# Fused forgetting attention and channel mix on one core: PSUM copies moved to ScalarE, and every slot ordered by a list from an offline model

## The chip, the cores and the metric

The kernel runs on one core of a Trainium2 chip. The metric is device time in microseconds (us): the median of several executions. The profile's span, from the first to the last instruction, is 1 to 2 us shorter than the time. Executions are compared only where they ran at about the same granted clock, the share of full speed at which TensorE was allowed to run (the fast state), and each kernel's runs are interleaved with runs of the kernel before on the same chip.

## The reference

Eight batches, eight heads, 576 positions, head size 64. A causal attention with a forget gate feeds a channel mix of 512 to 1024 to 512.

```python
scores = scale * np.matmul(q, k.transpose(0, 1, 3, 2))
cum = np.cumsum(np.log(np.clip(f, 0.0001, 1.0)), axis=-1)
scores = np.where(causal, -1e9, scores + cum[..., :, None] - cum[..., None, :])
attn = softmax(scores);  x = (attn @ v), heads side by side          # (8, 576, 512)
x_prev = x shifted by one position
xk = mu_k * x + (1 - mu_k) * x_prev;   xr = mu_r * x + (1 - mu_r) * x_prev
k = np.maximum(xk @ w_k, 0.0)
return sigmoid(xr @ w_r) * ((k * k) @ w_v)
```

## The kernel before

The order of instructions on each engine is the order in which the program writes them: nothing is rescheduled afterwards. Work goes in **slots**, one for each of the 32 pairs of heads (four pairs make a batch), and three more to empty the pipeline. A slot computes the scores and exponentials of its own pair, transposes q and k of the next one, casts those of the one after, sums the denominators of the previous pair, multiplies the values of a pair that lies three slots back, and runs key, gate and value units of the channel mix of an earlier batch between them.

Three scarce things tie the engines together: two score buffers in PSUM (`sc`, which also take the transposes), three general PSUM buffers (`mm`, for values, key, gate and value units), and three buffers `rb` for the normaliser, which travels through DRAM.

```python
sc_ring = Ring(2, [P, 2, 512], F32, "sc", scp)
mm_ring = Ring(3, [P, 512], F32, "mm", mmp)
rb_ring = Ring(3, [P, 2, S], F32, "rb")
...
def transposes(Pi, parts=(range(NC),)):         # TensorE, then the copy out of PSUM
    tp = sc_ring().bitcast(BF16)
    ...
            if Pi < RUNS and lo == 0:           # first six pairs: a strided copy
                nc.vector.tensor_copy(t[:, :, 0:4 * P].rearrange(...), tp[:, :, 0:4 * P].rearrange(...))
                lo = 4 * P
            if lo < hi:
                nc.vector.tensor_copy(t[:, :, lo:hi], tp[:, :, lo:hi])
...
def spread_norm(g):                             # R -> DRAM -> broadcast into rb
    scr = scr_ring()
    nc.sync.dma_start(out=scr..., in_=R...)
    rb = rb_ring()
    for half in range(2):
        for hh in range(2):
            nc.sync.dma_start(out=rb[...], in_=scr[2 * half + hh, 0:2, :].unsqueeze(0).to_broadcast([D, 2, HQ]))
...
def values(Pi, half):                           # TensorE into mm, then the product x = mm * rb
    ...
    nc.vector.tensor_tensor(out=xs[Pi % NX][...], in0=nm[:, 0:HQ], in1=rbs[Pi][...], op=ALU.mult)
...
def shift(Pi):                                  # the token shift: three VectorE instructions in SBUF
    nc.vector.tensor_sub(diff, x[:, 1:S + 1], x[:, 0:S])
    for dst, mu in ((xks[b], mu_k_sb), (xrs[b], mu_r_sb)):
        nc.vector.scalar_tensor_tensor(out=dst[:, p, :], in0=diff, scalar=mu[:, p:p + 1],
                                       in1=x[:, 0:S], op0=ALU.mult, op1=ALU.add)
...
def key_unit(b, hf, fb):                        # TensorE into mm, relu on ScalarE, square on VectorE
    kp = mm_ring()
    ...
    nc.scalar.activation(rel, kp[:, :HB], func=AF.Relu)
    nc.vector.tensor_mul(rsq[b][:, fb, hf * HB:(hf + 1) * HB], rel, rel)
...
def value_unit(b, t0):                          # TensorE into mm, product with the gate on VectorE
    ...
    nc.vector.scalar_tensor_tensor(out=res, in0=gates.pop((b, t0)), scalar=1.0, in1=vp, op0=ALU.add, op1=ALU.mult)
```

GpSimd casts q and k (`cast_pair`, and once a batch `cast_tails` for the last 64 positions), weights v with the gates (`vw_pair`, once a batch `vw_tail`) and masks. From slot 6 on, every slot has this one order:

```python
scores_and_masks(s, 0); run_gv(value_unit); transposes(s + 1)
run_keys(nk[0]); scores_and_masks(s, 1); cast_ahead(s)
denominators(s - 1); attend(Pi)                 # values of the pair three back
weigh(Pi); norm(...)                            # norm and its spreading in even slots
run_keys(nk[1]); spread_norm(...); shifted(Pi)
run_gv(); ...                                   # gate and value units
```

The softmax here doesn't subtract the row's maximum and nothing guards it: scores larger than these inputs give would overflow.

## Time and profile before

Before: 332.34 us, median of three runs (331.99 to 333.09). The span of its profile is 331.3 us.

I use one ruler: the start of each of the 32 groups of transposes on TensorE, numbered from 0. Between group 9 and group 31 every kernel of this study runs the same units (85 key units, 24 gate and value pairs, 22 slots of attention; the kernels with lists run six score matmuls more, about 0.5 us), so that stretch can be compared directly. I call it the **steady stage**; groups 1 to 9 are the **warm-up**, group 31 to the end the **drain**.

| stage of before | us |
|---|---|
| to group 1 | 13.5 |
| warm-up, groups 1 to 9 | 54.4 |
| steady, groups 9 to 31 | 197.8 |
| drain | 65.7 |

The busy times by stretch, before. The first column is the stretch in us from the span's start; then its length and the busy time of each engine with the count of its instructions; the last three are the granted clock of TensorE, the share of the DMA engines and GB/s.

```profile
core 0: us, PE busy (x) PEld busy (x) DVE busy (x) ACT busy (x) POOL busy (x), PEclk, DMA share, GB/s
13.50:67.87 54.37, 39.23 (x417) 24.26 (x418) 36.47 (x64) 32.06 (x49) 38.55 (x71) 0.94 0.88 170
67.87:265.63 197.76, 178.42 (x1852) 103.98 (x1852) 153.45 (x278) 116.35 (x198) 111.86 (x193) 0.99 0.76 171
```

Read the second row as a balance: 197.8 us long, TensorE busy for 178.4, so idle for 19.3.

VectorE's costliest SBUF work, before, by shape; the two numbers after the bar are us busy in all and ns of one.

```profile
L419 DVE TENSOR_TENSOR relusq<-rel 128x288 bf16<-128x288 bf16 x128 | 59.1, 484 | 12.1 <-ACT rel L418 10.2
L403 DVE SCALAR_TENSOR_TENSOR xk<-diff,mu_k_sb,x 128x576 bf16<-128x576 bf16 x32 | 28.5, 890 | 1.1
L401 DVE TENSOR_TENSOR diff<-x 128x576 bf16<-128x576 bf16 x32 | 18.2, 570 | 0.1
```

All three have two inputs in SBUF. Undisturbed, with no GpSimd instruction beside them, they take 0.31, 0.82 and 0.45 us (medians in this trace); their means here are well above that, which matters later.

### The profile page before, as it was taken

The page shows a single profiled execution, that of the slowest core. Times are in us where ns is not written, and L with a number is a line of the kernel's source. Part 1 is how long each engine was busy: PE and PEld are TensorE (multiplying, and loading weights), DVE is VectorE, ACT ScalarE, POOL GpSimd, SP SyncE. Part 2 cuts the span into 40 slices and gives each one's busy share as a digit, 9 for nine tenths or more (in the row PEclk, how much of TensorE's full clock was granted, in tenths as well). Part 3 has the DMA queues.
Part 4 walks back from the last instruction along what each step waited for, and adds up shares of the span by engine and source line. Part 5 has one row for each costly group of instructions (what it writes and reads, how often), then busy time and mean ns, then how long its engine had stood idle before and what let it go on. Part 6 is the DMA issues. An engine that isn't in the chain of part 4 may idle for free.

```text
span 331.3 us, 7464 instructions
## 1 busy us (share of the span) xinstructions
PE 278.4 (84%) x2741; PEld 162.8 (49%) x2741; DVE 235.2 (71%) x443; ACT 179.3 (54%) x304; POOL 165.3 (50%) x298
## 2 busy tenths in 40 slices
PE   1477668769979889899979897998889897989995
PEld 0235345445545535455545554554455554654552
DVE  4746567996888659777888778685888785677531
ACT  1655347656646646475746565575656574332541
POOL 6269655984684618445664547264745456000000
PEclk9999789999999979999999999999999999999999
DMA  8998997394968494946876696819595615041012
GB/s 180 239 206 174 189 202 133 95 204 125 217 156 209 115 214 111 256 93 164 213 188 157 157 220 165 228 55 217 137 240 109 163 55 168 32 153 64 34 63 96
DMA packets 123172, 51.33 MB, mean 155 GB/s; under 512 B 104384, under 2 KB 117952, under 8 KB 123136
## 3 DMA queue, kind: packets, MB, share of 16 engines
q1 hardware_dynamic: 120160, 47.70, 62.6%
q0 software_dynamic: 2096, 2.62, 4.8%
q10 hardware_dynamic: 880, 0.54, 0.7%
q8 instruction: 21, 0.34, 0.4%
q14 instruction: 15, 0.12, 0.1%
HBM read 41.96 MB, written 11.50 MB: 161 GB/s over the span
## 4 chain that ended last, share of the span: by engine, by line
PE 52%; DVE 21%; DMA 17%; SPq 4%; issue 3%; ACT 1%; POOL 1%; ACTq 0%; DVEq 0%; POOLq 0%
PE mm L426 21%; DMA rb<-scr 11%; PE mm L414 10%; PE mm L378 6%; PE sc L296 5%; SPq L349 4%; PE sc L229 4%; DMA scr<-R 4%; PE den L327 4%; DVE relusq L419 3%; DVE x L385 3%; DVE xr L403 2%; DVE qkT L237 2%; DVE qkT L233 2%; DMA rb<-in_f_dram 2%
## 5 line engine op out<-in xcount | busy, mean ns | idle before, releaser
L309 POOL TENSOR_SCALAR_AFFINE_SELECT a<-a 128x256 bf16<-128x256 bf16 (+1 forms) x160 | 73.7, 483 | 113.8 <-ACT a L302 108.8
L302 ACT ACTIVATE a<-sc 128x1024 bf16<-128x1024 f32 (+1 forms) x128 | 101.4, 836 | 19.1 <-PE sc L296 17.9
L418 ACT ACTIVATE rel<-mm 128x288 bf16<-128x288 f32 x128 | 52.5, 410 | 77.0 <-PE mm L414 73.6
L414 PE MATMUL mm<-xk,wk_sb 128*128 128x288 bf16 x512 | 74.1, 286 | 3.9 <-DVE xk L403 1.7
L419 DVE TENSOR_TENSOR relusq<-rel 128x288 bf16<-128x288 bf16 x128 | 59.1, 484 | 12.1 <-ACT rel L418 10.2
L426 PE MATMUL mm<-wv_sb,relusq 128*128 128x512 bf16 x256 | 62.4, 385 | 3.4 <-DVE relusq L419 3.0
L385 DVE TENSOR_TENSOR x<-mm,rb 128x288 bf16<-128x288 f32 x64 | 29.3, 461 | 41.1 <-PE mm L378 17.8
L414 PEld LDWEIGHTS <-wk_sb 128*128 128x128 bf16 x512 | 46.7, 98 | 19.4 <-issue 5.8
L296 PE MATMUL sc<-qkT 64*128 64x64 bf16 (+4 forms) x384 | 39.3, 293 | 18.5 <-DVE qkT L237 17.6
L440 ACT ACTIVATE th<-mm 128x512 f32<-128x512 f32 x36 | 21.5, 597 | 40.1 <-PE mm L426 34.2
L447 DVE SCALAR_TENSOR_TENSOR res<-th,mm 128x512 f32<-128x512 f32 x36 | 24.6, 682 | 24.7 <-ACT a L302 10.0
L426 PEld LDWEIGHTS <-relusq 128*128 128x128 bf16 x256 | 23.7, 99 | 35.1 <-issue 6.4
L426 PE MATMUL mm<-wr_sb,xr 128*128 128x512 bf16 x128 | 32.8, 379 | 7.2 <-DVE x L385 7.2
L296 PEld LDWEIGHTS <-qkT 64*128 64x128 bf16 x384 | 16.3, 96 | 45.3 <-issue 39.8
L211 POOL TENSOR_TENSOR vw<-vf,wbf 128x512 bf16<-128x512 f32 x32 | 34.3, 1072 | 1.5 <-DMA vf<-in_v_dram 1.5
L378 PE MATMUL mm<-a,vw 128*64 128x288 bf16 (+3 forms) x448 | 29.0, 269 | 1.0 <-DVE x L385 0.5
L403 DVE SCALAR_TENSOR_TENSOR xk<-diff,mu_k_sb,x 128x576 bf16<-128x576 bf16 x32 | 28.5, 890 | 1.1
L403 DVE SCALAR_TENSOR_TENSOR xr<-diff,mu_r_sb,x 128x576 bf16<-128x576 bf16 x32 | 27.9, 873 | 0.0
L327 PE MATMUL den<-a,E 128*2 128x288 bf16 (+4 forms) x512 | 22.7, 258 | 0.6 <-DVE E L268 0.5
L237 DVE COPY qkT<-sc 128x1280 bf16<-128x1280 bf16 (+1 forms) x32 | 22.8, 713 | 0.4 <-PE sc L229 0.4
L378 PEld LDWEIGHTS <-vw 128*64 128x64 bf16 x448 | 19.4, 113 | 7.5 <-issue 1.6
L426 PEld LDWEIGHTS <-xr 128*128 128x128 bf16 x128 | 12.4, 97 | 19.2 <-issue 9.1
(63 smaller groups left out, 242.7 us busy)
## 6 DMA issues: line engine op xcount, KB each, us to landing
out_dram<-res SPq DMA_DIRECT2D x36, 256.0 KB, 3.3
vf<-in_v_dram SPq DMA_DIRECT2D x64, 128.0 KB, 3.6
rb<-scr SPq DMA_DIRECT2D x56, 144.0 KB, 3.4
qf<-in_q_dram SPq DMA_DIRECT2D x52, 128.0 KB, 3.7
kf<-in_k_dram SPq DMA_DIRECT2D x52, 128.0 KB, 3.7
scr<-R SPq DMA_DIRECT2D x14, 144.0 KB, 1.7
qf<-in_q_dram SPq DMA_DIRECT2D x6, 256.0 KB, 3.4
kf<-in_k_dram SPq DMA_DIRECT2D x5, 256.0 KB, 4.1
```

The lines of the kernel that those rows point to most:

```text
L211: nc.gpsimd.tensor_tensor(out=vw[Pi % NV], in0=vf[Pi % NV], in1=wbf[:, :4, 2 * Pi:2 * Pi + 2].unsqueeze(3).to_broadcast([P, 4, 2, D]), op= ...
L296: nc.tensor.matmul(sc[:, hh, w:w + n], lhsT=t[lo:lo + D, 1, kb * P:(kb + 1) * P], rhs=t[lo:lo + D, 0, q0:q0 + n], start=True, stop=True)
L302: nc.scalar.activation(out=a[:, :, off:off + w], in_=sc[:, :, 0:w], func=AF.Exp, scale=SCALE)
L309: nc.gpsimd.affine_select(out=v_, in_=v_, compare_op=ALU.is_ge, fill=0.0, base=0, pattern=[[0, 2], [1, n]], channel_multiplier=-1)
L327: nc.tensor.matmul(den[r0:r0 + 2, o:o + n], lhsT=E[:, kb, 2 * h:2 * h + 2], rhs=a[:, hh, col:col + n], start=(Pi % 2 == 0 and kb == 0), st ...
L378: nc.tensor.matmul(nm[hh * D:(hh + 1) * D, o:o + n], lhsT=t[:, kb, hh, :] if kb < 4 else tl[:, 2 * p + hh, :], rhs=a[:, hh, col:col + n], ...
L385: nc.vector.tensor_tensor(out=xs[Pi % NX][:, 1 + o:1 + o + HQ], in0=nm[:, 0:HQ], in1=rbs[Pi][:, o:o + HQ], op=ALU.mult)
L403: nc.vector.scalar_tensor_tensor(out=dst[:, p, :], in0=diff, scalar=mu[:, p:p + 1], in1=x[:, 0:S], op0=ALU.mult, op1=ALU.add)
L414: nc.tensor.matmul(kp[:, :HB], lhsT=wk_sb[:, db, fb * P:(fb + 1) * P], rhs=xks[b][:, db, hf * HB:(hf + 1) * HB], start=(db == 0), stop=(db ...
L418: nc.scalar.activation(rel, kp[:, :HB], func=AF.Relu)
L419: nc.vector.tensor_mul(rsq[b][:, fb, hf * HB:(hf + 1) * HB], rel, rel)
L426: nc.tensor.matmul(ps, lhsT=tiles[b][:, i, t0:t0 + P], rhs=w[:, i, :], start=(i == 0), stop=(i == n - 1))
```

## The change

There are three parts. The copy of transposed q and k out of PSUM goes from VectorE to ScalarE. The order within a slot is no longer one fixed sequence but a list of letters: one list for each of the first eleven slots, four that repeat, one for the drain; the lists come from an offline model of the engines. And at the start the gates are loaded first, their clamp stands ahead of the casts, and only the tails of the first two heads are loaded and cast before the first transposes.

```diff
+    nc.scalar.dma_start(out=lf, in_=f_bh[:, :])
     load(q, qf[0], 0)
     load(k, kf[0], 0, nc.scalar)
-    load_tail(0, 0)
-    load_tail(1, 0, nc.scalar)
-    nc.scalar.dma_start(out=lf, in_=f_bh[:, :])
+    load_tail(0, 0, hs=(0, 2))
+    load_tail(1, 0, nc.scalar, hs=(0, 2))
     load_qk(1)
+    load_tail(0, 0, hs=(2, H))
+    load_tail(1, 0, hs=(2, H))
...
             if Pi < RUNS and lo == 0:
-                nc.vector.tensor_copy(t[:, :, 0:4 * P].rearrange("p i (j c) -> p i j c", c=4),
+                nc.scalar.copy(t[:, :, 0:4 * P].rearrange("p i (j c) -> p i j c", c=4),
...
             if lo < hi:
-                nc.vector.tensor_copy(t[:, :, lo:hi], tp[:, :, lo:hi])
+                nc.scalar.copy(t[:, :, lo:hi], tp[:, :, lo:hi])
...
-    cast_pair(0)
     nc.vector.tensor_scalar(lf, lf, scalar1=1e-4, scalar2=1.0, op0=ALU.max, op1=ALU.min)
     nc.scalar.activation(out=lf, in_=lf, func=AF.Ln)
+    cast_pair(0)
...
+    FIRST = ( ...eleven lists... 
+        "T G S0 c K3 S1 D W N G A P H G",
+        ... )
+    ROUND = (
+        "S0 V G T V K2 S1 c G A K2 D W N P H R G",
+        "S0 V K3 V T D c K1 S1 V G A H R W",
+        "S0 G T D K2 S1 A N c K2 P W G H R",
+        "S0 V T G K3 A D S1 G c K1 W H R",
+    )
+    DRAIN = "D V W K4 A N K4 H G G G P R"
-    WEIGHTS = (1, 3, 4)
+    WEIGHTS = (1, 3, 5)
...
+    def step(s, op, x):          # one branch for each letter
...
+        for op in (FIRST[s] if s < len(FIRST) else ROUND[s % PRW] if s < NP else DRAIN).split():
+            step(s, op[0], int(op[1:]) if op[1:] else None)
```

The letters that the argument needs: S0 and S1 are the two halves of the scores with exponentials and masks, T the transposes and their copy, D denominators, A the values and their products, N the normaliser and P its trip through DRAM, H the token shift, K2 two key units, V a value unit, G the next gate or value unit, R the gate and value units left over; c the casts and W the weighting of v, both on GpSimd.

## The prediction

> **What bounds the kernel now.** I read the page first (busy shares, slices, chain), then the waits, then the groups by shape, then the engines' timelines from 0 to 70 us and from 127 to 163 us. From the page of the kernel before, busy shares, two slice rows and the chain by engine:
>
> ```profile
> PE 278.4 (84%) x2741; PEld 162.8 (49%) x2741; DVE 235.2 (71%) x443; ACT 179.3 (54%) x304; POOL 165.3 (50%) x298
> ...
> PE   1477668769979889899979897998889897989995
> ...
> DMA  8998997394968494946876696819595615041012
> ...
> PE 52%; DVE 21%; DMA 17%; SPq 4%; issue 3%; ACT 1%; POOL 1%; ACTq 0%; DVEq 0%; POOLq 0%
> ```
>
> TensorE leads, yet only half of the last-ending chain is its own work: VectorE and the round trip of the normaliser through DRAM take most of the rest, ScalarE almost nothing. The first six slices (50 us) are a stage of their own: TensorE at 4 to 8 tenths, the DMA engines at 8 to 9.
>
> 84% overstates TensorE. From the timelines of a dense stretch, back to back: a group of ten transposes takes 0.56 us, the two halves of the scores 0.54 and 0.36, denominators 0.58, values 0.83, a key unit 0.49 (the chain has eight of its matmuls in 0.98), a gate block 0.86, a value block 1.73. I took the start of each of the 32 transpose groups in TensorE's timeline as a clock of the slots. Group 9 starts at 67.87 and group 31 at 265.63: 197.8 us for 22 slots, 9.0 each. Inside lie 22 x 2.87 (transposes, scores, denominators, values), 85 key units x 0.49 and 24 gate and value pairs x 2.59 (three of them straddle two batches and run as column halves side by side: 16 of those matmuls take 1.85): 63.1 + 41.7 + 62.9 = 167.7 us. So **30 us, 1.37 per slot, are lost in the steady stage**. The fastest full slots do show it possible: 142.15 to 149.76 is 7.61 us without a gap.
>
> Where they are lost, from the waits (waiter, released by: us in total, times, longest):
>
> ```profile
> PE sc L296 <- DVE qkT L237: 17.6, 15, 2.9
> DVE x L385 <- DMA rb<-scr: 17.5, 15, 2.3
> PE mm L426 <- DVE x L385: 7.6, 9, 2.0
> DVE rb L245 <- DMA rb<-in_f_dram: 3.6, 1, 3.6
> ```
>
> The first is the copy of transposed q and k out of PSUM: two score buffers exist, the transposes occupy one, and the last small score piece has to wait until VectorE has emptied it. The timelines of VectorE and of TensorE around 133 us show why VectorE is late:
>
> ```profile
> 131.45 0.95 DVE L403 SCALAR_TENSOR_TENSOR xr<-diff,mu_r_sb,x 128x576 bf16<-128x576 bf16 x1
> 132.32 0.68 DVE L447 SCALAR_TENSOR_TENSOR res<-th,mm 128x512 f32<-128x512 f32 x1
> 132.92 0.81 DVE L237 COPY qkT<-sc 128x1280 bf16<-128x1280 bf16 x1
> ```
> ```profile
> 133.79 0.20 PE L296 MATMUL sc<-qkT 64*128 64x64 bf16 x2 [1.11 <-DVE qkT L237]
> ```
>
> The transposes were done at 130.4; the copy stood behind the token shift and an output product in VectorE's queue for 2.5 us, and TensorE idled 1.11 us.
>
> At the start, the clamp of the gates stands on VectorE ahead of the same copy and waits for its load:
>
> ```profile
> 8.74 0.45 DVE L245 TENSOR_SCALAR rb<-rb 64x576 f32<-64x576 f32 x1 [3.61 <-DMA rb<-in_f_dram]
> ...
> 9.12 1.21 DVE L233 COPY qkT<-sc 128x1024 bf16<-128x1024 bf16 x1
> ```
>
> The transposes had ended at 5.8, so about 3.3 us of the first 9 are this clamp.
>
> **What the Trainium skill says.** "Perfetto Trace Analysis", section Identifying the Most-Contended Engine: matmul busy time is no measure of headroom because matmuls are pipelined. The trace agrees: a 512-column matmul is shown as 0.38 us, but 16 of them take 3.45 us, 0.216 each. That is why I used spacing, not busy share. "ScalarE: Activation LUTs", section What ACT_TABLE_LOAD costs: an activation with immediate operands takes 186 ns + 0.833 ns per element, and neighbours overlap by some 93 ns. The trace agrees: 1023 ns for 1024 elements, 410 for 288, 274 for 128. "SBUF — State Buffer", section Who interferes with whom: a VectorE instruction with two SBUF inputs contends with GpSimd, one with at most one SBUF input does not, outside two-port modes. The trace agrees in part: the square of the keys takes 0.31 us at best and 0.48 on average. So the moved copy, whose input is in PSUM, is not what GpSimd suffers from, and I count no gain there.
>
> **The change part by part.**
>
> (1) *Copies to ScalarE.* VectorE loses 26 x 0.81 + 6 x 1.21 + 6 x 0.28 = 30 us, from 235 to 205. ScalarE gains 26 copies of 1280 elements (186 + 1066 = 1.25 us, estimate by the ScalarE page; its own rows give 1.23) and six pairs of 1024 and 256 (1.02 + 0.40, taking the strided read as free): 32.5 + 8.5 = 41 us, from 179 to 220. Each copy is longer by 0.4 us, but it no longer waits behind 2.5 us of token shift; it waits behind exponentials instead. Per steady slot ScalarE has 3.34 (exponentials) + 4 x 0.41 + 9/8 x 0.60 + 1.25 = 6.9 us, VectorE about 6.5, TensorE 4.83 + 9/8 x 2.59 = 7.7. TensorE stays the longest, with ScalarE now close behind.
>
> (2) *Operation lists.* The order of instructions shows the same units on TensorE, moved. In the steady slots the transposes come earlier and key units, values or gates stand between them and the second half of the scores, so the copy has 1 to 3 us of cover. The values that need a freshly spread normaliser come after more TensorE work: before, some 5.5 us passed between the norm and its use (147.3 to 152.8); in the new odd slot two value blocks, four key units, transposes, denominators and half of the scores lie between, and in the slot after the norm in mid-slot about 7, against a DRAM trip of 7 to 8 us (1.75 to store, 2 to issue, 3.5 to load). Of the 1.37 us lost per slot I expect half back, a judgement: the first three waits listed above sum to 43 us over the whole run, and each shrinks rather than goes. 22 x 0.69 = **15 us**.
>
> (3) *Warm-up, first exponential to group 9.* Groups 1 to 6 start at 13.5 and 50.0: 7.3 us per slot. ScalarE would be busy 3.34 + 1.42 + 0.82 (spreading on chip) = 5.6, GpSimd 5.0, so neither permits 5. TensorE's waits for the copy in this stretch sum to 0.85 + 1.04 + 1.50 + 2.94 + 2.56 + 0.59 = 9.5 us. The DMA engines were full here (1.0 or more of their time in the windows from 20 to 50 us), though the third weight now leaves one slot later. I take 5 of 9.5: **5 us**.
>
> (4) *Start.* The gates are loaded first, only two heads of the tails are needed, and the clamp comes ahead of the casts. Other loads landed 3.3 us after issue, so the clamp ends near 4.5, casts near 5.4, transposes 6.3, ScalarE's copies near 7.9. Then the second table load, which the before kernel hid beside copying, comes in series (1.28 us). First exponential near 9.3 instead of 11.93: **2.5 us**.
>
> (5) *Drain.* From group 31 to the end 65.7 us; its units are the same number (36 keys, 12 pairs, the last values) and sum to 54, plus 4 for the last product and store. The order changes a little: **1 us**.
>
> The sum is 15 + 5 + 2.5 + 1 = 23.5, so 332.3 - 23.5 = 308.8. An order computed from modelled durations loses some of its fit on the chip, so I keep nine tenths: 311.
>
> **The rivals.** *ScalarE becomes the bound.* Exponentials, relu, tanh and copies share one in-order queue; key units need relu to free one of three PSUM buffers. For it: 6.9 of 7.7 us per slot, and a copy ahead of three relus. Against it: 54% busy before. If it holds, half of (2) is lost: about 318. *DMA holds the warm-up and the rb round trip.* For it: full DMA engines to 50 us, chains through rb; a faster slot asks for the same bytes sooner. Against: hardly any wait there names a q, k or v load (2.2, 1.1 and 1.5 us). Then (3) is nothing and (2) shrinks: about 317. *The lists fit better than I allow*, steady slots at 8.1 us: (2) gives 20 us, about 304. *Nothing gained*: copies return as equal waits on ScalarE; only the start remains, 328.
>
> **Range and chances.** The two bad cases together (318 and 317, each 6 to 7 above 311) give near 323 and the good one 304; I set 302 to 322. I give 89% to faster, since a gain under 6.6 us would need (2) and (3) both almost to fail; 9% to the same, 2% to slower.
>
> **What would show it.** Right: the first exponential near 9.3 us; the copy rows on ScalarE at about 1.25 us; VectorE near 205 and ScalarE near 220 us busy; waits of scores on the copy under 6 us in total; group 9 near 60 us; groups 9 to 31 some 182 to 186 us apart. Wrong: long waits of key matmuls on relu or of transposes on exponentials (ScalarE the bound), products waiting for rb as long as before, masks or casts waiting on loads, or strided copies well above 1.02 us.

## The result and the profile after

The changed kernel takes **319.46 us**, median of four runs (318.76 to 319.84), against 332.16 for the kernel before in the same rounds (331.64 to 333.09). Ratios in this document are the mean time of one kernel's fast runs over the mean of the other's fast runs of the same rounds, so not quite the ratio of the medians: 0.9612, 95% interval 0.9585 to 0.9640. It is faster by 3.9%, within the predicted range; the predicted gain was 21.3 us, the measured one 12.7.

From the page of the kernel after: busy shares, TensorE and DMA slices, chain by engine.

```profile
PE 277.0 (87%) x2741; PEld 162.3 (51%) x2741; DVE 218.5 (69%) x407; ACT 213.0 (67%) x342; POOL 174.5 (55%) x298
...
PE   2675887598998998999988998999979999999994
...
DMA  8999959596968495928788696929695526141102
...
PE 62%; DVE 18%; ACT 7%; DMA 5%; issue 4%; POOL 2%; SPq 1%; DVEq 0%; ACTq 0%; POOLq 0%
```

VectorE lost 17 us, ScalarE gained 34. The DMA engines' part of the chain fell from 17% to 5%, but VectorE's only from 21% to 18%, although it gave its copies away.

The busy times by stretch, after, the same columns as before:

```profile
10.68:61.40 50.72, 36.87 (x411) 23.17 (x411) 28.63 (x49) 38.80 (x60) 39.25 (x68) 0.97 0.95 182
61.40:253.73 192.33, 179.55 (x1858) 104.43 (x1858) 143.73 (x255) 141.16 (x222) 120.11 (x195) 0.99 0.76 177
```

| stage | before | after | gain | predicted gain |
|---|---|---|---|---|
| to group 1 | 13.5 | 10.7 | 2.8 | 2.5 |
| warm-up | 54.4 | 50.7 | 3.7 | 5 |
| steady | 197.8 | 192.3 | **5.4** | **15** |
| drain | 65.7 | 63.4 | 2.3 | 1 |
| span | 331.3 | 317.1 | 14.2 | 23.5 |

Everything but the steady stage came out close. There TensorE's busy time is the same (178.4, 179.6), and its idle time went from 19.3 to 12.8 us. What it idles for, in the waits of TensorE over the steady stage (us in total, times, longest), before and then after:

```profile
PE sc L296 <- DVE qkT L237: 7.8, 8, 2.0
PE mm L426 <- DVE x L385: 5.1, 7, 2.0
PE mm L426 <- DVE relusq L419: 3.0, 3, 1.0
PE mm L414 <- DVE xk L403: 1.7, 2, 0.9
```
```profile
PE mm L418 <- DVE res L451: 5.6, 7, 1.2
PE sc L233 <- ACT a L306: 3.4, 4, 1.0
PE sc L300 <- ACT qkT L241: 2.0, 2, 1.0
PE mm L418 <- DVE xk L407: 1.3, 4, 0.3
```

The change did what it was made for: the scores' wait for the copy fell from 7.8 to 2.0 us, and the gate and value units no longer wait for products (5.1) or squares (3.0). But a wait that the kernel before did not have leads the list: key units waiting for an output product, `res`, 5.6 us. The timeline of the kernel after from 154 to 161 us shows where it is made (start, duration, engine, operation; the bracket is idle time and releaser):

```profile
154.52 0.76 POOL L204 CAST kb<-kf 128x512 bf16<-128x512 f32 x1
...
155.23 1.24 POOL L212 CAST tail<-tail_f 64x512 bf16<-64x512 f32 x2
...
155.36 1.42 DVE L405 TENSOR_TENSOR diff<-x 128x576 bf16<-128x576 bf16 x1
...
156.44 1.23 POOL L221 TENSOR_TENSOR tail<-tail_f,wbf 64x512 bf16<-64x512 f32 x1
156.81 2.48 DVE L407 SCALAR_TENSOR_TENSOR xk<-diff,mu_k_sb,x 128x576 bf16<-128x576 bf16 x1
...
160.09 0.68 DVE L451 SCALAR_TENSOR_TENSOR res<-th,mm 128x512 f32<-128x512 f32 x1
...
160.82 0.40 PE L418 MATMUL mm<-xk,wk_sb 128*128 128x288 bf16 x2 [1.19 <-DVE res L451]
```

The three instructions of the token shift take 0.45, 0.82 and 0.82 us undisturbed. Here, while GpSimd casts and weighs, `diff` takes 1.42 and `xk` 2.48 us; `xk` ends at 159.29, 0.6 us after GpSimd's weighting of v (157.64 to 158.68, among the lines left out). The output product behind it ends at 160.77; it held one of the three `mm` buffers, and the key unit that needed that buffer starts 0.05 us later after 1.19 us of idling. The same 1.19 us are lost just before 125, 195 and 231 us: once in every four slots, after the slot whose list ends in "N c K2 P W G H R", where the casts, the weighting and the tails of a batch fall beside the shift.

The groups say the same of the whole run (same columns as before):

```profile
L423 DVE TENSOR_TENSOR relusq<-rel 128x288 bf16<-128x288 bf16 x128 | 50.2, 408 | 30.2 <-ACT rel L422 28.6
L407 DVE SCALAR_TENSOR_TENSOR xk<-diff,mu_k_sb,x 128x576 bf16<-128x576 bf16 x32 | 34.7, 1084 | 1.1
L405 DVE TENSOR_TENSOR diff<-x 128x576 bf16<-128x576 bf16 x32 | 27.2, 852 | 0.4
```

`diff` rose from 570 to 852 ns and `xk` from 890 to 1084, `xr` from 873 to 1002; the squares fell from 484 to 408. The contention was moved from the squares to the shift. A count over the same trace shows that GpSimd is the cause: with no GpSimd instruction beside them, no `diff`, `xk`, `xr` or square took more than 457, 819, 814 or 310 ns; beside GpSimd work other than masks they took up to 2078, 2485, 2445 and 1864. In the kernel before, 4 of the 32 `diff` ran beside such work, after the change 24.

Two lines on the parts that went as predicted, ScalarE's copy by shape and then its timeline at the start:

```profile
L241 ACT COPY qkT<-sc 128x1280 bf16<-128x1280 bf16 x26 | 31.9, 1227 | 12.0 <-PE sc L233 11.3
```
```profile
8.31 1.28 ACT L306 ACT_TABLE_LOAD   x1
9.60 1.02 ACT L306 ACTIVATE a<-sc 128x1024 bf16<-128x1024 f32 x1
```

### The profile page after: what moved, and what is told of

It is laid out like the page before. It is cut to its first block, busy times and chain, and to the rows that moved or that the text cites. A ratio compares the mean times of both kernels' runs of the same rounds, so it can differ in the third digit from the quotient of the medians.

```text
span 317.1 us, 7414 instructions
## 1 busy us (share of the span) xinstructions
PE 277.0 (87%) x2741; PEld 162.3 (51%) x2741; DVE 218.5 (69%) x407; ACT 213.0 (67%) x342; POOL 174.5 (55%) x298
## 4 chain that ended last, share of the span: by engine, by line
PE 62%; DVE 18%; ACT 7%; DMA 5%; issue 4%; POOL 2%; SPq 1%; DVEq 0%; ACTq 0%; POOLq 0%
PE mm L430 20%; PE mm L418 16%; PE mm L382 7%; PE sc L300 6%; PE den L331 5%; PE sc L233 4%; PE mm L434 4%; ACT a L306 3%; DVE xr L407 3%; DVE diff L405 3%; DVE relusq L423 3%; DVE res L451 3%; DMA kf<-in_k_dram 2%; DVE xk L407 2%; DMA rb<-scr 1%
## 5 line engine op out<-in xcount | busy, mean ns | idle before, releaser
L313 POOL TENSOR_SCALAR_AFFINE_SELECT a<-a 128x256 bf16<-128x256 bf16 (+1 forms) x160 | 79.8, 520 | 92.9 <-ACT a L306 81.0
L306 ACT ACTIVATE a<-sc 128x1024 bf16<-128x1024 f32 (+1 forms) x128 | 100.1, 841 | 14.7 <-PE sc L300 14.6
L423 DVE TENSOR_TENSOR relusq<-rel 128x288 bf16<-128x288 bf16 x128 | 50.2, 408 | 30.2 <-ACT rel L422 28.6
L430 PE MATMUL mm<-wv_sb,relusq 128*128 128x512 bf16 x256 | 60.7, 380 | 0.0
L389 DVE TENSOR_TENSOR x<-mm,rb 128x288 bf16<-128x288 f32 x64 | 28.6, 459 | 30.7 <-PE mm L382 14.2
L300 PE MATMUL sc<-qkT 64*128 64x64 bf16 (+4 forms) x384 | 37.9, 290 | 8.9 <-ACT qkT L241 5.9
L241 ACT COPY qkT<-sc 128x1280 bf16<-128x1280 bf16 (+1 forms) x32 | 34.2, 1067 | 12.5 <-PE sc L233 11.7
L407 DVE SCALAR_TENSOR_TENSOR xk<-diff,mu_k_sb,x 128x576 bf16<-128x576 bf16 x32 | 34.7, 1084 | 1.1
L407 DVE SCALAR_TENSOR_TENSOR xr<-diff,mu_r_sb,x 128x576 bf16<-128x576 bf16 x32 | 32.1, 1002 | 0.0
L405 DVE TENSOR_TENSOR diff<-x 128x576 bf16<-128x576 bf16 x32 | 27.2, 852 | 0.4
L233 PE MATMUL sc<-ident,qb 128*128 128x128 bf16 x128 | 13.2, 229 | 12.8 <-ACT a L306 6.5
```

Source lines behind the costliest of these rows:

```text
L241: nc.scalar.copy(t[:, :, lo:hi], tp[:, :, lo:hi])
L300: nc.tensor.matmul(sc[:, hh, w:w + n], lhsT=t[lo:lo + D, 1, kb * P:(kb + 1) * P], rhs=t[lo:lo + D, 0, q0:q0 + n], start=True, stop=True)
L306: nc.scalar.activation(out=a[:, :, off:off + w], in_=sc[:, :, 0:w], func=AF.Exp, scale=SCALE)
L313: nc.gpsimd.affine_select(out=v_, in_=v_, compare_op=ALU.is_ge, fill=0.0, base=0, pattern=[[0, 2], [1, n]], channel_multiplier=-1)
L430: nc.tensor.matmul(ps, lhsT=tiles[b][:, i, t0:t0 + P], rhs=w[:, i, :], start=(i == 0), stop=(i == n - 1))
```

## The experiments

Theory C (called P in the first texts): the lists run GpSimd's SBUF work beside the token shift, and what they gain elsewhere is paid back there. Rival theory S: ScalarE, with the copies added, has become the bound in the steady stage, so the lists would do better without the copies. Rival theory D: DRAM trips and loads hold the slots. The table has every run; "steady core" is the stretch from group 14 to group 30, sixteen slots away from warm-up and drain. All results agree with the reference except where stated. Medians are of all runs, ratios of the fast runs against the kernel before on the same chip. Stages and busy times come from one profile of each.

| kernel | warm-up | steady | drain | steady core | TensorE busy in it | idle in it | median us | ratio to before (95%) |
|---|---|---|---|---|---|---|---|---|
| before | 54.4 | 197.8 | 65.7 | 146.5 | 132.8 | 13.7 | 332.2 | 1 |
| after | 50.7 | 192.3 | 63.4 | 140.2 | 131.4 | 8.9 | 319.46 | 0.9612 (0.9585 to 0.9640) |
| after_again | 49.9 | 192.8 | 63.7 | 140.1 | 130.3 | 9.8 | 320.23 | 0.9696 (0.9653 to 0.9740) |
| copies_act | 53.0 | 191.5 | 65.7 | 140.9 | 131.3 | 9.6 | 327.53 | 0.9941 (0.9864 to 1.0018) |
| lists_dve | 55.2 | 198.3 | 63.3 | 142.2 | 131.1 | 11.1 | 329.15 | 0.9949 (0.9905 to 0.9992) |
| start_only | 54.0 | 194.8 | 65.4 | 143.7 | 130.4 | 13.3 | 328.94 | 0.9957 (0.9896 to 1.0018) |
| start_copies | 56.9 | 190.0 | 66.0 | 140.4 | 131.2 | 9.2 | 326.72 | 0.9899 (0.9849 to 0.9949) |
| no_tails | 51.2 | 189.4 | 62.6 | 135.6 | 131.0 | 4.6 | 315.38 | 0.9538 (0.9496 to 0.9581) |
| early2 | 52.9 | 191.4 | 62.9 | 137.6 | 130.1 | 7.4 | 319.46 | 0.9647 (0.9581 to 0.9713) |
| early2_np | 51.3 | 193.7 | 64.0 | 142.2 | 131.7 | 10.6 | 322.02 | 0.9718 (0.9661 to 0.9775) |
| np_all | 49.4 | 191.6 | 62.0 | 139.2 | 129.9 | 9.3 | 319.78 | 0.9689 (0.9634 to 0.9744) |
| np_tails_act | 48.4 | 193.2 | 62.5 | 139.0 | 131.4 | 7.6 | 319.52 | 0.9659 (0.9615 to 0.9703) |
| np_sq_mix | 51.8 | 190.1 | 64.6 | 136.4 | 131.8 | 4.6 | 319.03 | 0.9615 (0.9565 to 0.9665) |
| early2_np_mix | 50.5 | 193.0 | 65.5 | 139.1 | 132.4 | 6.7 | 322.16 | 0.9708 (0.9658 to 0.9758) |

A caution first. The unchanged kernel after was measured twice, and its two ratios (0.9612 and 0.9696) have intervals that do not overlap. So ratios of different calls are comparable to about 1%, and only kernels of one call are compared more closely: copies_act, lists_dve, start_only and early2 in the first; after_again, start_copies, early2_np and np_all in the second; no_tails, np_tails_act and np_sq_mix in the third; early2_np_mix stood alone in a fourth. Eight of the fourteen profiles (after_again, copies_act, lists_dve, start_only, start_copies, early2, early2_np, np_all) lack some 13 matmul records in the steady core, so their TensorE busy time may be short, and their idle time too long, by 1 us.

### What each part is worth

**copies_act**: the kernel before, with nothing but the copies on ScalarE.

```diff
-                nc.vector.tensor_copy(t[:, :, lo:hi], tp[:, :, lo:hi])
+                nc.scalar.copy(t[:, :, lo:hi], tp[:, :, lo:hi])      # and the strided one
```

> The kernel before with only the copies moved to ScalarE, old order and old start. Theory P: the copies cost waits of scores of 17.6 us in the kernel before, of which a third comes back: 325 to 329 us. Theory S: the old order gives the copy no cover and ScalarE's queue puts it behind two exponentials: 331 to 335 us.

Measured: 0.9941 (327.5 us, in theory P's range), a gain of 0.6% that the interval does not separate from none.

**lists_dve**: the kernel after, with the copies put back on VectorE (the lists and the start stay).

```diff
-                nc.scalar.copy(t[:, :, lo:hi], tp[:, :, lo:hi])
+                nc.vector.tensor_copy(t[:, :, lo:hi], tp[:, :, lo:hi])   # and the strided one
```

> The changed kernel with one part undone: the transposed q and k are copied out of PSUM by VectorE again, under the new lists and the new start. Theory P (the steady stage's missing gain, 192.3 us for groups 9 to 31 where 182 to 186 were predicted, goes to the token shift on VectorE being stretched by GpSimd work that the lists put beside it): ScalarE is not the bound, so giving it 41 us less work brings nothing and giving VectorE 30 us more costs 2 to 5 us: 321 to 325 us. Theory S (ScalarE, now 67% busy, is the bound): 314 to 318 us, faster than the change.

Measured: 0.9949. Theory S falls: if ScalarE were the bound, taking 40 us of copies off it should have kept the gain or raised it; instead nearly all of it is gone, and the steady stage (198.3 us) is as long as that of the kernel before. Theory P's range was missed too: it expected 2 to 5 us to be lost, not nearly all. TensorE's waits in this steady stage show both costs at once: 7.5 us for the copy and 5.9 for `res`.

**start_only**: the kernel before, with the new start alone (gates first, clamp ahead of the casts, tails of two heads first).

```diff
-    cast_pair(0)
     nc.vector.tensor_scalar(lf, lf, scalar1=1e-4, scalar2=1.0, op0=ALU.max, op1=ALU.min)
     nc.scalar.activation(out=lf, in_=lf, func=AF.Ln)
+    cast_pair(0)                       # and the loads as in the change
```

> The kernel before with only the new start: gates loaded first, clamp ahead of the casts, tails in two parts. Copies stay on VectorE. First exponential near 9.6 us instead of 11.9; both theories expect that lead to be kept to the end in part: 329 to 330.5 us. If the DMA engines hold the warm-up, it is swallowed: 332 us.

Measured: 0.9957. Group 1 starts at 11.5 us instead of 13.5; the gain fits that, and the interval includes none.

**start_copies**: start and copies, the old order of the slots. So it is the kernel after without the lists. **after_again** is the kernel after, unchanged, on the same chip.

```diff
 (start_only) +
-                nc.vector.tensor_copy(t[:, :, lo:hi], tp[:, :, lo:hi])
+                nc.scalar.copy(t[:, :, lo:hi], tp[:, :, lo:hi])      # and the strided one
```

> The kernel before with the new start and the copies on ScalarE: everything of the change but the operation lists. Theory L0 (the lists bring little: in the trace of the copies alone, groups 9 to 31 of the transposes took 191.5 us under the old order, the changed kernel 192.3): ratio 0.965 to 0.978, within 1.5% of the changed kernel. Theory L1 (new order and moved copies need each other, as lists alone gave 0.995 and copies alone 0.994): ratio 0.982 to 0.992.

> The changed kernel itself again, as the standard on this chip for the other three: ratio to the kernel before 0.955 to 0.968, as on record.

Measured: 0.9899 and 0.9696 (the second a little above what was expected of it). Side by side, the lists are worth 2.0% once the copies are on ScalarE. Put together:

| | copies on VectorE | copies on ScalarE |
|---|---|---|
| old order, old start | 1 | 0.9941 |
| old order, new start | 0.9957 | 0.9899 |
| lists, new start | 0.9949 | 0.9612, 0.9696 |

Without the lists the copies are worth 0.6%, with them 2.5 to 3.4%; without moved copies the lists are worth nothing. The parts need each other. The stages tell how, with one profile of each kernel. **In these profiles the steady stage owes its gain to the copies alone**: 197.8, 194.8 and 198.3 us with the copies on VectorE, the last of them with the lists; with the copies on ScalarE 191.5 and 190.0 in the old order, 192.3 and 192.8 with the lists. The lists give the drain 2 us with or without moved copies (63.3 to 63.7 against 65.4 to 66.0), and the warm-up some 4 us where the copies are on ScalarE too: nine profiles with both lie between 48.4 and 52.9 us, the five others between 53.0 and 56.9. That last difference is only partly one of order: TensorE's granted clock in the warm-up varied from 0.88 (lists_dve) to 0.98 (np_all) between profiles. At nearly equal clocks, the three kernels with both at 0.93 took 48.4 to 51.3 us and the three without the lists at 0.94 took 53.0 to 54.4, so some 2 us or more are not the clock's. (In the steady stage of lists_dve, the clock between groups 9 and 14 was 0.93, against 1.00 in start_only; not all of the 3.5 us between these two is the lists'.)

So why do the lists bring nothing in the steady stage? In the old order with moved copies (start_copies) products wait for the normaliser's trip:

```profile
DVE x L389 <- DMA rb<-scr: 20.0, 18, 2.0
```

With the lists that is 14.0 us; from 88 to 254 us it is 4.5, against 12.2 in start_copies. The lists did shorten what they were meant to shorten, and something else took the room: TensorE's waits in the steady stage sum to 12.7 us in start_copies (products 7.8, `xk` 3.9, exponentials 1.0) and to 12.8 in the kernel after (`res` 5.6, exponentials 3.9, the copy 2.0, `xk` 1.3).

### Is it the contention?

**no_tails**: wrong (relative error 1.43). From the fifth batch on GpSimd does not cast the tails, and from the fourth it does not weigh them; stale data is used. TensorE, VectorE and ScalarE do the same work in the same order.

```diff
-        if Pi % PRW == 0:
+        if Pi % PRW == 0 and Pi // PRW < 3:
             vw_tail(Pi // PRW)
...
-            if (s + 2) % PRW == 0:
+            if (s + 2) % PRW == 0 and (s + 2) // PRW < 4:
                 cast_tails((s + 2) // PRW)
```

> Wrong results on purpose. The changed kernel, its lists untouched, but GpSimd neither casts the tails of q and k nor weights that of v after the third batch: 2.5 to 3.7 us of GpSimd work less in every fourth slot, where the changed kernel's difference takes 1.42 us and its first mix 2.48. Theory C (what the lists lose in the steady stage is VectorE blocked by GpSimd work, so it goes when that work goes, and was only pushed onto the squared keys when the casts were moved earlier): the two slow slots of eight, 12.05 and 10.47 us, fall to about 10.3 and 8.8, groups 14 to 30 take 133 to 137 us instead of 140.2, ratio 0.95 to 0.96 where the changed kernel had 0.961 and 0.970. Rival R (the three PSUM buffers or the DRAM trip hold these slots in any case): groups 14 to 30 stay within 1 us of 140, ratio as the changed kernel.

Measured: 0.9538, and the steady core shrinks from 140.2 to 135.6 us. TensorE's waits in the steady core, and VectorE's on the normaliser:

```profile
PE mm L430 <- DVE x L389: 2.0, 2, 1.1
PE sc L233 <- ACT a L306: 1.9, 2, 1.0
PE mm L418 <- DVE res L451: 0.5, 2, 0.3
DVE x L389 <- DMA rb<-scr: 12.7, 9, 2.4
```

The wait on `res` falls from 5.3 us (kernel after, the same sixteen slots) to 0.5, and the longest `xk` there from 2.48 to 1.03 us. VectorE's own program was not touched. This confirms theory C: 13 instructions fewer on GpSimd (285 instead of 298) set free 4.6 us in sixteen slots. A rival, that GpSimd's shorter queue let its masks come earlier, does not fit: in the kernel after, neither TensorE nor VectorE waited for GpSimd in the steady core. It also shows what stands behind: products now wait 12.7 us for the normaliser, against 3.4 in the kernel after.

### Can a list avoid it?

**early2**: in the slot with the tails, casts and weighting stand at the start of the slot instead of beside the shift.

```diff
-        "S0 G T D K2 S1 A N c K2 P W G H R",
+        "S0 c W G T D K2 S1 A N K2 P G H R",
```

> The changed kernel with one list edited: in the third list of the round, where GpSimd casts tails as well, its casts and its weighting of v are issued right after the first half of the scores, when GpSimd was idle, instead of beside the token shift. Theory P: in these slots the difference takes 0.45 us instead of 1.42 and the first mix 0.82 instead of 2.48, the key matmuls' wait for the output product (5.3 us in the steady stage) is gone, five slots gain some 1 to 2 us each: 311 to 315 us. Theory S: ScalarE's work and order are as before, 318 to 320 us.

Measured: 0.9647 (319.5 us where theory P expected 311 to 315), no gain over the kernel after within 1%. The stall of the shift is gone (wait on `res` 0.5 us), and the steady core is 2.7 us shorter, but products wait for the normaliser 9.3 us instead of 3.4 in the steady core, and a pair of squares now falls beside GpSimd's work: one takes 2.28 us.

**early2_np**: the same, and the normaliser and its trip (N P) also earlier.

```diff
-        "S0 G T D K2 S1 A N c K2 P W G H R",
+        "S0 c W G T D N P K2 S1 A K2 G H R",
```

> The third list of the round edited twice: GpSimd's casts and weighting early, as in the run before, and the norm with its store and spread moved right behind the denominators, some 3 us earlier. Theory D (with the stretching of the token shift gone, the same slots waited for the normaliser's trip through DRAM instead: 4.5 us of such waits in the steady stage rose to 10.5): the waits of products on rb fall under 4 us, groups 9 to 31 take 183 to 188 us, ratio 0.945 to 0.957. Rival (the DMA queue is simply late whatever the order): rb waits stay near 10 us and the ratio stays at 0.96 to 0.97.

Measured: 0.9718 (after_again's 0.9696). The wait for the normaliser is down to 2.6 us, but now the squares meet GpSimd (one takes 2.73 us), products queue behind them, and TensorE waits for products 6.7 us, up to 2.2 at once. The steady core is 142.2 us, longer than before this edit.

**np_all**: all four lists with casts and weighting first, and N P early.

```diff
+        "S0 c W V G T V K2 S1 D N P G A K2 H R G",
+        "S0 c W V K3 V T D K1 S1 V G A H R",
+        "S0 c W G T D N P K2 S1 A K2 G H R",
+        "S0 c W V T G K3 A D S1 G K1 H R",
```

> As the run before, in all four lists of the round: casts and weighting of v right behind the first half of the scores, the norm and its spread early in both even slots and in slot 8. If the token shift's contention and the DRAM trip are what is left in every slot: ratio 0.935 to 0.952 and mean durations of the shift's three instructions back near 0.57, 0.89 and 0.87 us. If the casts only move the contention to the squared keys: the same as the run before, 0.95 to 0.96.

Measured: 0.9689 against after_again's 0.9696, the same; both expected ranges were missed. Between 88 and 254 us the shift is at its fastest (medians 452, 819 and 815 ns), but some squares take up to 1.45 us, and in the steady core TensorE waits 6.1 us for products that queue behind them. The contention was moved once more.

**np_tails_act**: np_all with the tails of q and k cast on ScalarE, to take two casts a batch off GpSimd.

```diff
-            eng = nc.vector if b == 0 else nc.gpsimd
-            eng.tensor_copy(tail[i][b % 2][:64, hs, :], tail_f[i][:, hs, :])
+            if b == 0: nc.vector.tensor_copy(...)
+            else:      nc.scalar.copy(...)
```

> Correct results. The version with casts, weighting and norm early in every list, and the casts of the tails of q and k on ScalarE instead of GpSimd (two of about 0.6 us per four slots). Theory C: 1.2 us of blocking less beside the squared keys in every fourth slot: 1 to 4 us faster than that version, ratio 0.955 to 0.965. Rival (ScalarE is too full by now): as that version or slower, 0.967 to 0.975.

Measured: 0.9659, the steady core 139.0 us (np_all 139.2). No gain; the pair casts and the weighting remain on GpSimd, but no run shows that they are why.

**np_sq_mix**: np_all, where the square is the product of the key unit in PSUM and its relu in SBUF (the same value), so that only one input is in SBUF.

```diff
-        nc.vector.tensor_mul(rsq[b][:, fb, hf * HB:(hf + 1) * HB], rel, rel)
+        nc.vector.tensor_mul(rsq[b][:, fb, hf * HB:(hf + 1) * HB], kp[:, :HB], rel)
```

> Correct results. The same version without the tail casts on ScalarE, but the squared key is taken as the PSUM value times its relu, so that VectorE has one SBUF input in it instead of two. Theory C by the Trainium skill's page on SBUF: the instruction no longer waits for GpSimd, all 128 take 0.35 to 0.47 us, none over 0.6. Its PSUM buffer is held until VectorE is done, though. If the blocking is the larger cost: ratio 0.945 to 0.96. If the three PSUM buffers are: waits of key matmuls on VectorE rise above 10 us and the ratio is 0.97 to 0.99.

Measured: 0.9615, between the two expected ranges. One view of one source line settles the mechanism: the squares from 88 to 254 us, shortest, median and longest in ns, in np_all and then in np_sq_mix.

```profile
L423 DVE TENSOR_TENSOR relusq<-rel x76: 287/310/1449, 91.0 to 248.9; 128x288 bf16<-128x288 bf16 x76
```
```profile
L423 DVE TENSOR_TENSOR relusq<-mm,rel x77: 418/457/459, 89.2 to 249.3; 128x288 bf16<-128x288 f32 x77
```

With one input in PSUM the square is slower at its median (457 against 310) and never blocked: its longest is 459 ns. The Trainium skill, "SBUF — State Buffer", section Who interferes with whom, says that a VectorE instruction with at most one SBUF input does not contend with GpSimd, outside two-port modes; this trace agrees. TensorE's idle time in the steady core falls to 4.6 us, as in no_tails, with right results. But the time hardly does: 0.9615 against np_tails_act's 0.9659, within their intervals. The warm-up is 51.8 us and the drain 64.6 in this profile, against 49.4 and 62.0 in that of np_all. That of np_all was its fastest run, at a granted clock of 0.98 in the warm-up against 0.90 here. Key units now hold their `mm` buffer until VectorE has squared, not only until the relu, but TensorE does not wait for a square in the steady core and only once, for 0.6 us, in the drain; why the drain is longer is not shown.

**early2_np_mix**: early2_np with that square, the lists otherwise those of the kernel after.

```diff
-        nc.vector.tensor_mul(rsq[b][...], rel, rel)
+        nc.vector.tensor_mul(rsq[b][...], kp[:, :HB], rel)      # and the one list of early2_np
```

> Correct results; the best that the earlier runs point to. The changed kernel with only its third list edited (casts, weighting, norm and spread early) and the squared key taken as the PSUM value times its relu. The edit of the list alone brought the slow slots from 12.05 and 10.47 us to 10.34 and 8.8, but blocked the squared keys for up to 2.9 us; with one SBUF input they are not blocked. Theory C: groups 14 to 30 take 133 to 136 us, the wait of key matmuls on VectorE is under 2 us there, ratio 0.945 to 0.958. If the PSUM buffers, now held through VectorE's queue, cost as much as the blocking did: 139 us or more and 0.962 to 0.972.

Measured: 0.9708, and 139.1 us for the steady core: the expected gain did not come, and both lie where the rival, PSUM buffers held through VectorE's queue, put them. (The 2.9 us of the expectation is not in the traces: the longest square took 2.28 us in early2 and 2.73 in early2_np.) No square is blocked, but values wait 4.2 us for squares to free an `mm` buffer, and products wait 12.8 us for the normaliser.

No version with right results beats the changed kernel beyond the 1% that separates its own two measurements.

## Why the prediction was right or wrong

**Right.** The verdict (faster) and the range. The first exponential: 9.3 predicted, 9.60 measured, against 11.93; the second table load does come in series. The copies: 1.25 us predicted, 1.227 measured, and 1.01 for the strided ones (1.02). ScalarE's busy time: 220 predicted, 213.0 measured; the rows of the copies sum to 40.3 us (41 predicted), but neighbouring activations overlap and the busy time rose by 33.7. The scores' waits on the copy over the whole run: under 6 predicted, 5.9 measured. (One reading was loose: the square's 0.31 us "at best" is its undisturbed median; the shortest took 0.27.) The warm-up gained 3.7 (5 predicted), and the scores' waits on the copy there fell from 9.8 to 4.0 us; part of the gain may be the clock. The drain gained 2.3 (1 predicted).

**Wrong in size: term (2), the steady stage**, 15 us predicted and 5.4 measured; it alone makes up the miss. Two steps in it failed.

The first is the pool: "30 us, 1.37 per slot, are lost in the steady stage". It was counted against the cheapest spacing of each unit, 167.7 us. The stretch view of the same profile has TensorE busy for 178.4 us, hence 19.3 idle. The timelines tell what the difference of 10.7 us is. First, 44 times a unit whose weights are a full 128x128 block is followed by one with a smaller block, and then takes some 0.1 us longer (a key unit 0.586 us before scores, 0.490 before another key unit): 4.2 us, which no filling of gaps gives back. The lists raise this to 56 times and 5.4 us. Second, where TensorE waits after a unit or inside it, the record of the last matmul before the wait is mostly 0.16 to 0.18 us longer, however long the wait (a key unit then shows 0.65 us): 4.7 us in 28 places before, about 4 after, which is idle time shown as busy. Two units between 118 and 121 us took 1.6 us more for no reason that I see. So some 24 us were idle, not 30, and half of that would have been 12 us.

The second is "Of the 1.37 us lost per slot I expect half back, a judgement: the first three waits listed above sum to 43 us over the whole run, and each shrinks rather than goes", with the sentence that closed the other door: "So the moved copy, whose input is in PSUM, is not what GpSimd suffers from, and I count no gain there". Of those 43 us only 25.5 lay in the steady stage (7.8, 12.6 and 5.1), and 9.5 of the first wait had already been used in term (3). And I treated contention as a constant because the copy is no part of it. But a new order changes which VectorE work runs beside GpSimd. By the waits of TensorE in the steady stage, the old ones shrank by 14.9 us (copy 7.8 to 2.0, products 5.1 + 1.0 to none, squares 3.0 to none), and 8.1 came back: `res` and `xk` behind a blocked shift (6.9 instead of 1.7), and exponentials (3.9 instead of 1.0). The gross gain happens to equal the predicted net one; less than half of it stayed. Undoing the blocking (no_tails) gives 4.6 us in sixteen slots, and no list that I wrote by hand gained as much: each passed the blocking to other instructions, or to the normaliser's trip, or to the `mm` buffers.

VectorE's busy time, 205 predicted and 218.5 measured, is the same miss: the shift's three rows grew by 19.4 us and the squares' shrank by 8.9. In no_tails VectorE is at 207.3.

**The rivals.** ScalarE as the bound: refuted by lists_dve; its trace in the changed kernel is 3.4 us of transposes waiting on exponentials. DMA holding the normaliser's trip: true of the old order, and again in some versions that take the blocking away (12.7 us in the steady core of no_tails, 9.3 in early2), but not where the norm comes early in all lists (1.8 in np_all); in the changed kernel it is 3.4.

**Open.** How much exactly of the warm-up's 3.7 us is order and how much is the granted clock (0.94 before, 0.97 after in the profiles shown). The products of slots 9 to 12 in the changed kernel still wait 9.7 us for a normaliser whose trip takes 8 us there with the DMA engines nine tenths busy; no run isolates those loads.

## What to carry to other kernels

An order computed from a model is only as good as what the model holds: if two engines slow each other when their work overlaps, the order decides where that cost falls, so look for instructions whose mean lies far above their fastest case and ask beside what they run. Before sizing a gain from idle time, set the sum of the best cases beside the busy time that the profile shows and account for the difference (here 30 and 19.3 us, and some 24 after the account), and count what takes the place of each wait removed. And test the parts alone and together: here the copies alone were worth 0.6% and the lists alone nothing, and the pair about 3%.

## What the Trainium skill lacked or had wrong

- "SBUF — State Buffer", section Who interferes with whom: the rule holds here; the page says that the loser is blocked for the whole instruction, but gives no measured times for instructions with two SBUF inputs. In these runs a 128x576 product-sum of 0.82 us took up to 4.03 (2.48 in the changed kernel), a 128x576 difference of 0.45 us up to 2.08, and a 128x288 square of 0.31 us up to 2.83 beside GpSimd; beside nothing but masks, no product-sum took more than 1.04. The square with one input in PSUM took at most 459 ns in all 256 cases of two kernels.
- "ScalarE: Activation LUTs", section What ACT_TABLE_LOAD costs: it counts a drain of about 1.38 us beside the load of 1.28. Here the load took 1.28 us (8.31 to 9.59), the copy ahead of it had ended at 8.29, and the exponential started at 9.60: no drain is seen.
- "Perfetto Trace Analysis", section Identifying the Most-Contended Engine: it warns that matmul busy time is a bad measure of headroom. The trace agrees, but the section puts no size on it. Here busy time in the steady stage lay 10.7 us above the sum of the cheapest spacings; 4.7 us of that were idle time shown as busy, and 4.2 us belonged to changes of the weights' shape.
